# An attention block with a gated block behind it: background work that waits for a time of the plan

## The chip, the cores and the metric

The kernel runs on one core of a Trainium2 chip. The metric is the time of one execution on the device, in microseconds (us). A core has five engines that run side by side, each with its own queue of instructions that it takes in order: TensorE (PE in the profile; its weight loads are listed apart, as PEld), VectorE (DVE), ScalarE (ACT), GpSimd (POOL) and SyncE (SP), which here issues all transfers (DMA). They wait for each other through semaphores. An instruction that waits at the head of its engine's queue holds all that stand behind it.

## The reference

One sequence of 2048 rows of 640 numbers (bf16) goes through attention and then through a gated block:

```python
x = A_x
h = x + _A_ref(_layernorm(x, axis=-1), A_wqkv, A_wo)
h2 = h + _B_ref(_layernorm(h, axis=-1), B_w_gate, B_w_up, B_w_down)
```

`_A_ref` makes queries, keys and values for 32 heads of 20 numbers, the softmax of `q k^T / sqrt(20)`, its product with the values, and the product of all heads with `wo` (640 x 640). `_B_ref` is `((x w_gate) * (x w_up)) w_down`, with 1728 columns between. `_layernorm` takes off the mean and divides by the root of the variance.

## The kernel before

Heads are taken in 8 groups of 4; a head has a slot of 32 partitions. Queries are taken in 4 blocks of 512, in passes "0", "1", "2", "3" (block 3 is partly split into two halves "A" and "B"). Keys and values come in 16 tiles of 128 rows, four tiles to a chunk, so 4 chunks.

**The main loop** goes over 683 score tiles of 1536 columns (three units of 512, each one head by one key tile). `emit_S` has TensorE multiply keys with queries into one of two score tiles `sc` (L456). ScalarE takes the exponential of the tile into one of six buffers `E` (L469). Where the plan finds VectorE free (`x_takes`), the exponential covers 1024 columns only and VectorE works out the last 512 in five instructions (`emit_x`, L494 to L505). `emit_AV` multiplies the finished exponentials with the values into the one accumulator `acc` (L631); at the end of a group VectorE copies it out (L642, L647).

**Other work of TensorE** is a list of jobs that share one work bank `mi`: a job's matmuls, then VectorE's copy out of the bank, then the next job. Jobs are projections of queries and keys (`job_proj`, copied by L286), values (`job_V`, copied by L248), transposes of normalized input (`T_of`, `job_lnT`, copied by L248), and, when a block of queries is done, its output product (`out_mm`), the second layer norm and the gated block. Where the plan finds TensorE idle, two filler matmuls are issued (`keep_warm`, L432).

**Who sets the order.** The program is written out by a planner that runs while the kernel is built. It keeps its own clocks: `at["pe"]` and `at["dve"]` are the times in ns at which it believes TensorE and VectorE to be, advanced by fixed costs for each job. Nothing of these clocks is left on the chip: what they set is the order of instructions in each engine's queue. `run_job` and `spare` decide after each tile which jobs and which background work go next.

**VectorE's background work** is the list `aux` of generators. `step_aux` runs the first of them to its next `yield` and adds the yielded cost to `at["dve"]`; only when it is finished does the next get a turn. `ensure_aux` drives the list until a named thing is done. In the list are:

- `gen_ln(ch)` for chunks 1 to 3: four statistics (L183, L184) of the chunk's input `xs`, the inverse root of the variance in small steps on POOL (`rstd_steps`, L189 to L214), a reciprocal on VectorE (L219), then four times subtract and multiply (L238, L239). Between POOL's steps and the reciprocal the generator yields 24 times a cost of 50 ns. A chunk's input must have been asked for (`while ch not in xs`); `xs` has two buffers, so chunk 3's load (L142) waits until chunk 1's transposes have read theirs.
- `load_wo`: for each of 8 groups, clear `wo[g]` (L789) and issue four transfers of 20 rows each (L793).
- later, `ln2_pieces` of the second layer norm.

**Sums.** After L642 copies a group's accumulator to `asb`, `norm` stores its row of sums to DRAM and reads it back in another shape (L537, L538); five tiles later `back` puts the reciprocal into VectorE's queue (L543), and stores and spreads the result (L545, L548); eight tiles on, POOL multiplies (L554). `later(n, fn)` is "n tiles from now".

**The order of jobs in a chunk** (the loop over `ch`): for chunks 1 to 3 four values, then the keys of head groups 1, 2, 3, with the next chunk's transposes between; the key of group 0 was made at the end of the chunk before. A chunk's group takes 5.33 tiles, so the key of group 1 is wanted about five tiles after the chunk begins.

Of the kernel before, what the change touches and what calls it, by code (L numbers as in the profile page):

```python
# [33 lines left out]
TPB = QB // P  # L34
# [20 lines left out]
EXP_NS, EXP_END, EXP_COL = 50, 166, 5 / 6  # L55
S_NS, S_EXP, SWITCH, LAT = 323, 500, 110, 150
TOL, LEAST, MARGIN = 200, 430, 100
X_LEAST, X_OUT = 3, 6
E_BUFS = 6
SHIFT = 1184.0  # L60
# [12 lines left out]
def kernel(  # L73
# [112 lines left out]
    def rstd_steps(mv, n, made, ve_=None):  # L186
        ve_ = ve_ or nc.vector
        mb = small.tile([P, n], BF16, name="mb")
        ve_.tensor_copy(mb[:], mv[:, :, 0])  # L189
        m32 = small.tile([P, n], F32, name="m32")  # L190
        ve_.tensor_copy(m32[:], mb[:])
        vb = small.tile([P, n], BF16, name="vb")
        ve_.tensor_copy(vb[:], mv[:, :, 1])
        ve = small.tile([P, n], BF16, name="ve")
        ve_.tensor_scalar_add(ve[:], vb[:], EPS_B)
        v = small.tile([P, n], F32, name="v")
        ve_.tensor_copy(v[:], ve[:])
        yield 1000 if ve_ is nc.vector else 50
        y = small.tile([P, n], F32, name="y")
        ve_.tensor_scalar(y[:].bitcast(I32), v[:].bitcast(I32), -0.5, float(0x5F3759DF), ALU.mult, ALU.add)  # L200
        t = small.tile([P, n], F32, name="nt")
        for k in range(3):
            ve_.tensor_tensor(t[:], y[:], y[:], ALU.mult)
            if ve_ is nc.gpsimd:
                ve_.tensor_tensor(t[:], t[:], v[:], ALU.mult)
                ve_.tensor_scalar(t[:], t[:], -0.5, 1.5, ALU.mult, ALU.add)
                ve_.tensor_tensor(y[:], t[:], y[:], ALU.mult)
            else:
                ve_.scalar_tensor_tensor(t[:], t[:], -0.5, v[:], ALU.mult, ALU.mult)
                ve_.scalar_tensor_tensor(y[:], t[:], 1.5, y[:], ALU.add, ALU.mult)  # L210
            if k != 2:
                yield (800, 600)[k] if ve_ is nc.vector else 50
        den = small.tile([P, n], BF16, name="den")
        ve_.tensor_tensor(den[:], v[:], y[:], ALU.mult)  # L214
        if ve_ is nc.gpsimd:
            for _ in range(24):
                yield 50
        r = small.tile([P, n], F32, name="rstd")
        nc.vector.reciprocal(r[:], den[:])  # L219
        made.append((m32, r))  # L220
        yield 1000 if ve_ is nc.vector else 200
# [2 lines left out]
        nc.vector.tensor_scalar(dst, src, m32[:, k:k + 1], r[:, k:k + 1], ALU.subtract, ALU.mult)  # L224

    lns = {}
    now = {"i": 0}
    at = {"pe": 0, "dve": 0, "mi": 0, "acc": 0, "slot": [0, 0], "exp": 0, "av": {}}

    def dve(ns):  # L230
# [128 lines left out]
    def later(n, fn):  # L359
        events.append((now["i"] + n, fn))  # L360
# [45 lines left out]
                raise RuntimeError(f"no job for {key}")  # L406

    def step_aux():
        while aux:
            try:  # L410
                at["dve"] += next(aux[0]) or 200
                return True
            except StopIteration:
                aux.popleft()
        return False

    def spare(until):
# [2 lines left out]
                break  # L420

    def ensure_aux(key):
        while key not in done:
            if not step_aux():
                raise RuntimeError(f"nothing makes {key}")

    COST = {"T": 300, "v": 680, "nf": 780}

# [101 lines left out]
    def norm(s, asb):  # L530
# [6 lines left out]
        nc.sync.dma_start(sums[:], asb[DH:P:SLOT, 0:w])  # L537
        nc.sync.dma_start(r16, sums[:].rearrange("j (c f) -> (j c) f", f=n))  # L538

        def back():  # L540
            ri = nrm.tile([P, n], F32, name="ri", tag=f"ri{n}")
            dve(240)
            nc.vector.reciprocal(ri[:], r16)  # L543
            scr = dram.tile([HPG, w], F32, name="scr", tag=f"scr{w}")
            nc.sync.dma_start(scr[:].rearrange("j (c f) -> (j c) f", f=n), ri[:])  # L545
            bc = nrm.tile([P, QB], F32, name="bc")
            for j in range(HPG):
                nc.sync.dma_start(bc[SLOT * j:SLOT * (j + 1), 0:w], scr[j:j + 1, :].to_broadcast([SLOT, w]))  # L548

            def mult():  # L550
                if b and ("om", b - 1) not in done:
                    later(1, mult)
                    return
                nc.gpsimd.tensor_tensor(On[g][:, c0:c0 + w], asb[:, 0:w], bc[:, 0:w], ALU.mult)  # L554
                done.add(("n", p, g))
            later(8, mult)
        later(5, back)

    def sums_on_pe(asb, w):
        ps = bank()  # L560
# [192 lines left out]
    for ch in range(NB):  # L753
        nxt = deque(range((ch + 1) * TPB, (ch + 2) * TPB) if ch + 1 < NB else [])

        def one_T():
            if nxt:
                t = nxt.popleft()
                add(("T", t), T_of(t))
        def values():  # L760
            for t in range(ch * TPB, (ch + 1) * TPB):
                add(("v", t, 0), job_V(t, 0))
        if ch:
            values()
        for g in range(1, G1):
            if ch == 0:
                add(("q", 0, g), job_proj(0, g, 0))
            add(("k", g, ch), job_proj(1, g, ch))
            if ch == 0 and g == 1:
                values()  # L770
            if g > 1:
                one_T()
        one_T()
# [13 lines left out]
    def load_wo():  # L787
        for g in range(NG):
            nc.vector.memset(wo[g][:], 0.0)  # L789
            yield 230  # L790
            for j in range(HPG):
                h = HPG * g + j
                nc.sync.dma_start(wo[g][SLOT * j:SLOT * j + DH, :], A_wo[DH * h:DH * h + DH, :])  # L793

    def make_identf():
        nc.vector.tensor_copy(identf[:], ident[:])
# [477 lines left out]
```

## Time and profile before

| | |
|---|---|
| median of 3 runs | 968.78 us (967.51 to 969.49) |
| the profiled execution | 966.26 us |
| its span, first to last instruction | 964.4 us |
| ScalarE busy | 899.1 us (93%) |
| TensorE busy | 845.2 us (88%) |
| VectorE busy | 604.3 us (63%) |
| POOL busy | 59.8 us (6%) |
| granted TensorE clock, mean | 0.980 |

In the profile's rows, `L469 ACT ACTIVATE E<-sc` is line 469, ScalarE, the operation, and the tile written and read. In groups there follow the count, the busy time, the mean of one in ns, and the idle time of the engine just before them with what ended it. In a timeline the row begins with start and length in us, and idle time stands in brackets. In a table of stretches the busy times of the engines are followed by the granted clock of TensorE (1.00 is full speed), the DMA engines' share and the bytes moved per second.

### The profile page before, as it was taken

The numbers are of one execution on the slowest core, as the hardware profiler recorded it, in microseconds if no ns is written. First come the engines' busy times: TensorE is split into PE (matmuls) and PEld (weight loads), VectorE is DVE, ScalarE is ACT, GpSimd is POOL, SyncE is SP. The second block draws the span as 40 slices with busy tenths as digits, with TensorE's granted clock in tenths as the row PEclk, the third lists the DMA queues.
The fourth block names the chain that finished last, engine by engine and source line by source line (L and its number), as shares of the span: only waits on it lengthen the run. The fifth ranks groups of instructions, "written<-read, shape, count | busy, mean of one in ns | idle before, by whom it ended". The sixth has DMA issues, their size and how long they took to land.

```text
span 964.4 us, 18116 instructions
## 1 busy us (share of the span) xinstructions
PE 845.2 (88%) x7237; PEld 328.4 (34%) x7237; DVE 604.3 (63%) x1219; ACT 899.1 (93%) x719; POOL 59.8 (6%) x155
## 2 busy tenths in 40 slices
PE   7778999878988899998898999998898899888897
PEld 5233332222223222331233222332332334435465
DVE  7664448867778787888877887878644322133242
ACT  6889999979999899999999999999999999999941
POOL 3220011000000000000000000000000000000000
PEclk9999999989999999997999999999899999999899
DMA  6000010010060122004021221000502000202310
GB/s 185 28 1 1 1 29 22 15 44 12 3 186 13 40 77 51 20 27 182 13 68 39 68 68 33 27 27 15 155 2 67 14 13 20 62 23 59 76 41 17
DMA packets 67818, 44.44 MB, mean 46 GB/s; under 512 B 18504, under 2 KB 63404, under 8 KB 67728
## 3 DMA queue, kind: packets, MB, share of 16 engines
q1 hardware_dynamic: 67728, 43.23, 16.2%
q8 instruction: 58, 0.95, 0.4%
q14 instruction: 32, 0.26, 0.1%
HBM read 35.91 MB, written 7.30 MB: 45 GB/s over the span
## 4 chain that ended last, share of the span: by engine, by line
ACT 48%; PE 25%; issue 17%; DVE 8%; POOL 1%; DMA 1%; SPq 0%; ACTq 0%; DVEq 0%; POOLq 0%
ACT E L469 48%; PE sc L456 6%; PE acc L631 4%; PE mi L968 3%; PE mi L279 3%; PE mi L432 2%; PE f L913 2%; PE f L968 1%; PE mi L913 1%; PE mi L293 1%; DVE kT L286 1%; DVE st L183 1%; PE mi L847 1%; DVE xt L504 1%; DVE qa L286 1%
## 5 line engine op out<-in xcount | busy, mean ns | idle before, releaser
L469 ACT ACTIVATE E<-sc 128x1536 bf16<-128x1536 f32 (+1 forms) x683 | 881.7, 1466 | 24.6 <-PE sc L456 18.5
L456 PE MATMUL sc<-qa,kT 32*128 32x512 bf16 x1536 | 204.5, 389 | 49.8 <-ACT E L469 42.3
L456 PEld LDWEIGHTS <-kT 32*128 32x128 bf16 x2432 | 85.5, 91 | 297.1 <-issue 258.1
L631 PE MATMUL acc<-E,vx 128*32 128x512 bf16 (+1 forms) x2331 | 171.9, 355 | 1.4 <-DVE asb L642 0.9
L279 PE MATMUL mi<-lnT,wp 128*128 128x512 bf16 x310 | 85.3, 386 | 16.6 <-DVE qa L286 10.7
L494 DVE TENSOR_SCALAR xv<-sc 128x512 f32<-128x512 f32 x101 | 69.6, 689 | 41.0 <-PE sc L456 40.2
L456 PE MATMUL sc<-qb,kT 32*128 32x256 bf16 (+1 forms) x896 | 69.8, 293 | 16.2 <-ACT E L469 15.0
L554 POOL TENSOR_TENSOR on<-asb,bc 128x512 bf16<-128x512 f32 (+1 forms) x30 | 34.6, 1153 | 716.5 <-DMA bc<-scr 430.9
L504 DVE SCALAR_TENSOR_TENSOR xt<-xm 128x512 f32<-128x512 int32 x101 | 76.7, 759 | 2.1
L499 DVE SCALAR_TENSOR_TENSOR xe<-xt,xv 128x512 int16<-128x512 f32 x101 | 70.8, 701 | 1.7
L505 DVE SCALAR_TENSOR_TENSOR xt<-xt,xm 128x512 f32<-128x512 f32 x101 | 69.9, 692 | 2.1
L631 PEld LDWEIGHTS <-vx 128*32 128x32 bf16 x2432 | 45.0, 96 | 67.2 <-issue 66.4
L968 PE MATMUL mi<-wd,hh 128*128 128x320 bf16 x364 | 63.7, 303 | 1.5 <-DVE xr L972 1.5
L432 PE MATMUL mi<-kT,ident 128*128 128x512 bf16 x196 | 61.6, 397 | 2.1 <-DVE ln2T L248 1.0
L968 PEld LDWEIGHTS <-hh 128*128 128x128 bf16 x448 | 38.8, 98 | 37.4 <-issue 25.2
L913 PE MATMUL mi<-ln2T,wg 128*128 128x512 bf16 (+1 forms) x170 | 47.6, 387 | 3.7 <-DVE u L248 3.5
L921 DVE TENSOR_TENSOR hh<-mi,u 128x512 bf16<-128x512 f32 (+1 forms) x42 | 28.8, 687 | 34.9 <-PE mi L913 34.7
L913 PE MATMUL mi<-ln2T,wu 128*128 128x512 bf16 (+1 forms) x170 | 46.3, 382 | 3.9 <-DVE hh L921 3.9
L248 DVE CAST u<-mi 128x512 bf16<-128x512 f32 (+1 forms) x42 | 28.9, 688 | 32.7 <-PE mi L913 32.6
L279 PEld LDWEIGHTS <-wp 128*128 128x128 bf16 x310 | 26.2, 97 | 62.0 <-issue 46.8
L503 DVE TENSOR_SCALAR xm<-xv 128x512 int32<-128x512 int32 x101 | 44.1, 436 | 0.6
L847 PE MATMUL mi<-wo,on 128*128 128x320 bf16 x224 | 38.8, 301 | 2.3 <-DVE xr L851 2.2
(150 smaller groups left out, 610.3 us busy)
## 6 DMA issues: line engine op xcount, KB each, us to landing
bc<-scr SPq DMA_DIRECT2D x100, 64.0 KB
wu<-in_B_w_up_dram SPq DMA_DIRECT2D x20, 320.0 KB
wg<-in_B_w_gate_dram SPq DMA_DIRECT2D x20, 320.0 KB
qsp<-qa SPq DMA_DIRECT2D x8, 384.0 KB
xr<-in_A_x_dram SPq DMA_DIRECT2D x16, 160.0 KB
out_dram<-xr SPq DMA_DIRECT2D x14, 160.0 KB
wd<-in_B_w_down_dram SPq DMA_DIRECT2D x13, 160.0 KB
xs<-in_A_x_dram SPq DMA_DIRECT2D x3, 640.0 KB
```

The source lines that it names most:

```text
L279: nc.tensor.matmul(ps[:], lhsT=wslice(m, g, c), rhs=lnT[:, c, ch * QB:(ch + 1) * QB], start=(c == 0), stop=(c == KT - 1))
L432: nc.tensor.matmul(ps[:], lhsT=ident[:], rhs=kT[0][:, 0:BANK], start=True, stop=True)
L456: nc.tensor.matmul(sc[:, o:o + w], lhsT=kT[g][SLOT * j:SLOT * (j + 1), kt * P:(kt + 1) * P], rhs=q_of(g, b, c0, w)[SLOT * j:SLOT * (j + 1) ...
L469: exps = nc.scalar.activation(e[:, 0:n_act], sc[:, 0:n_act], ACT.Exp, bias=EXP_BIAS, scale=SM_SCALE)
L494: took = nc.vector.tensor_scalar(v[:], ps, X_SCALE, X_BASE, ALU.mult, ALU.max)
L499: nc.vector.scalar_tensor_tensor(e[:], t[:], X_C, v[:], ALU.add, ALU.add)
L504: (700, lambda: nc.vector.scalar_tensor_tensor(t[:], m[:], X_A, m[:], ALU.mult, ALU.mult)),
L505: (700, lambda: nc.vector.scalar_tensor_tensor(t[:], t[:], X_B, m[:], ALU.add, ALU.mult)),
L631: nc.tensor.matmul(acc["t"][SLOT * j:SLOT * (j + 1), 0:w], lhsT=vx[kt][:, VS * h:VS * h + SLOT], rhs=e, start=(acc["n"][j] == 0), stop=(ac ...
L847: nc.tensor.matmul(ps[:, 0:HALF], lhsT=on[g][:, t * P:(t + 1) * P], rhs=wo[g][:, cs], start=(g == 0), stop=(g == NG - 1))
L913: nc.tensor.matmul(ps[0:M, 0:n], lhsT=st["w", fp][k][:, c, f2 * P:f2 * P + M], rhs=st["ln2T"][:, c, c0:c0 + n], start=(c == 0), stop=(c == ...
L968: nc.tensor.matmul(ps[:, 0:HALF], lhsT=st["hh"][f][0:K, t * P:(t + 1) * P], rhs=late["Wd"][f][0:K, cs], start=(f == 0), stop=(f == 2 * FP ...
```

## The change

Four edits, all in the planner:

1. A generator of background work may yield `WAIT`, "not yet". `step_aux` then gives the next generator in the list a turn instead of stopping at the first. `ensure_aux` sets `now["forced"]`, under which no generator waits. The 24 yields before the reciprocal of the first layer norm become a wait until `at["pe"]` has passed the time of POOL's last step by `ROOT_NS` = 5000.
2. `load_wo` waits `WO_NS` = 1500 of the plan's time after each group of four transfers.
3. `back` is called four tiles after the sums are stored, and puts itself off by a tile at a time until `at["pe"]` has passed the store by `SUMS_NS` = 6000.
4. In chunks 1 to 3 two values stand ahead of the key of group 1, and two behind it.

```diff
+WO_NS, SUMS_NS, ROOT_NS = 1500, 6000, 5000
...
         if ve_ is nc.gpsimd:
-            for _ in range(24):
-                yield 50
+            due = max(at["dve"], at["pe"]) + ROOT_NS
+            while at["pe"] < due and not now["forced"]:
+                yield WAIT
...
     def step_aux():
-        while aux:
+        for gen in list(aux):
             try:
-                at["dve"] += next(aux[0]) or 200
+                c = next(gen)
+                if c == WAIT:
+                    continue
+                at["dve"] += c or 200
                 return True
             except StopIteration:
-                aux.popleft()
+                aux.remove(gen)
         return False
...
     def ensure_aux(key):
+        now["forced"] = True
         while key not in done:
             if not step_aux():
                 raise RuntimeError(f"nothing makes {key}")
+        now["forced"] = False
...
+        due = at["dve"] + SUMS_NS
+
         def back():
+            if at["pe"] < due and now["i"] < n_tiles:
+                later(1, back)
+                return
...
-        later(5, back)
+        later(4, back)
...
-        def values():
-            for t in range(ch * TPB, (ch + 1) * TPB):
+        def values(k=0, n=TPB):
+            for t in range(ch * TPB + k, ch * TPB + n):
                 add(("v", t, 0), job_V(t, 0))
         if ch:
-            values()
+            values(0, 2)
         for g in range(1, G1):
...
-            if ch == 0 and g == 1:
-                values()
+            if g == 1:
+                values(2 if ch else 0)
...
                 nc.sync.dma_start(wo[g][SLOT * j:SLOT * j + DH, :], A_wo[DH * h:DH * h + DH, :])
+            due = at["pe"] + WO_NS
+            while at["pe"] < due and not now["forced"]:
+                yield WAIT
```

2 lines of the change are left out of this document (1 added, 1 removed).

## The prediction

> **What bounds the kernel now.** I read the page first (busy shares and the chain of waits), then ScalarE's instructions by shape, the timeline of ScalarE for its gaps, and SyncE, VectorE and TensorE where the gaps lie.
>
> ```profile
> PE 845.2 (88%) x7237; PEld 328.4 (34%) x7237; DVE 604.3 (63%) x1219; ACT 899.1 (93%) x719; POOL 59.8 (6%) x155
> ...
> ACT 48%; PE 25%; issue 17%; DVE 8%; POOL 1%; DMA 1%; SPq 0%; ACTq 0%; DVEq 0%; POOLq 0%
> ```
>
> ```profile
> L469 ACT ACTIVATE E<-sc 128x1536 bf16<-128x1536 f32 x581 | 804.9, 1529 | 17.6 <-PE sc L456 14.3 <-PE acc L631 1.7
> L469 ACT ACTIVATE E<-sc 128x1024 bf16<-128x1024 f32 x102 | 113.2, 1110 | 7.0 <-PE sc L456 4.1 <-PE acc L631 2.6
> ```
>
> ScalarE is busy 93% of the span. Its 683 exponentials (581 whole, 102 with a third taken over by VectorE) run back to back almost everywhere; before them it was idle 24.6 us in all. I number them from 0. So a change can win only what closes a gap of ScalarE, or takes columns off it. Its timeline shows where the large gaps are (start, length, engine, instruction; in brackets the idle time before it):
>
> ```profile
> 28.66 2.79 ACT L469 ACTIVATE E<-sc 128x1536 bf16<-128x1536 f32 x2 [1.73 <-PE acc L631]
> 32.96 14.88 ACT L469 ACTIVATE E<-sc 128x1536 bf16<-128x1536 f32 x11 [1.50 <-PE sc L456]
> 48.67 6.82 ACT L469 ACTIVATE E<-sc 128x1536 bf16<-128x1536 f32 x5 [0.83 <-PE sc L456]
> 59.73 21.60 ACT L469 ACTIVATE E<-sc 128x1536 bf16<-128x1536 f32 x16 [4.24 <-PE sc L456]
> ```
>
> ```profile
> 209.47 3.88 ACT L469 ACTIVATE E<-sc 128x1024 bf16<-128x1024 f32 x3 [3.96 <-PE sc L456]
> 214.60 2.36 ACT L469 ACTIVATE E<-sc 128x1536 bf16<-128x1536 f32 x2 [1.25 <-PE sc L456]
> 217.32 18.44 ACT L469 ACTIVATE E<-sc 128x1536 bf16<-128x1536 f32 x14 [0.36 <-PE sc L456]
> ```
>
> ```profile
> 319.69 3.71 ACT L469 ACTIVATE E<-sc 128x1024 bf16<-128x1024 f32 x3 [2.11 <-PE acc L631]
> ```
>
> Two groups can be touched by the edits: 8.30 us before exponentials 8, 10, 21 and 26 (start), and 5.57 us between 205.5 and 217.3 us (the output weight).
>
> **Part 1, the output weight's transfers and the read-back.** SyncE's queue, then VectorE and TensorE at the second group:
>
> ```profile
> 191.21 11.93 SPq L793 DMA_DIRECT2D wo<-in_A_wo_dram  x32
> 203.24 0.51 SPq L537 DMA_DIRECT2D sums<-asb  x1
> ```
>
> ```profile
> 206.68 0.25 DVE L543 RECIPROCAL ri<-sums_all 128x16 f32<-128x16 f32 x1 [4.45 <-DMA sums_all<-sums]
> 206.85 0.69 DVE L286 TENSOR_SCALAR qa<-mi,shift_row 128x512 bf16<-128x512 f32 x1
> ```
>
> ```profile
> 207.59 1.23 PE L279 MATMUL mi<-lnT,wp 128*128 128x512 bf16 x4 [3.78 <-DVE qa L286]
> ```
>
> The reader is to see a line of four. The 32 transfers hold SyncE for 11.93 us; the sums that L537 stores are issued only after them, at 203.24; the reciprocal that reads them back stands in VectorE's queue and waits 4.45 us; behind it stands the copy that frees TensorE's one work bank, so TensorE waits 3.78 us and ScalarE 3.96 us. In the order of the changed kernel's built instructions the sums stand behind 4 of the 32 transfers instead of all, and the reciprocal follows five exponentials behind the store (in the order before the two stand within one). Store to landing took 3.44 us (203.24 to 206.68), five exponentials take over 6 us (14 in 18.44 us above), so the wait should be gone: **-3.96 us**. The two gaps of 1.25 and 0.36 us behind it lie in and after a stretch in which TensorE had half its clock, quoted under the rivals, that began when it had stood still; without the stop I take them as gone too: **-1.61 us**. Bounds for this part: -5.57, and 0 if another wait takes the place.
>
> The transfers stay 32 and the clearing of wo 8 memsets; only their spread changes (the last group is issued about exponential 145 instead of 135). Their first reader stands near exponential 194 in the changed order, so that costs nothing; without that cover one late group would be a wait of four issues, 11.93 / 8 = 1.49 us. On SyncE, 28 of the 32 come behind the stored sums, and the read-back results (L545, L548, five issues) stand between groups; one group ahead is 1.49 us, below the slack of the multiply on POOL eight exponentials later. Of the other 33 read-backs no reciprocal waits for its DMA in the trace of before; they move by at most four exponentials. I take 0 for them, between 0 and one more wait like the 4.45.
>
> **Part 2, roots and second keys at the start.** VectorE before exponentials 8 to 10 with the first half of a normalizing pair, the copies of chunk 1's first and second keys with a statistic between, and one value's matmuls on TensorE:
>
> ```profile
> 26.14 0.49 DVE L248 CAST vx<-mi 128x320 bf16<-128x320 f32 x1 [0.93 <-PE mi L293]
> 29.52 0.18 DVE L219 RECIPROCAL rstd<-den 128x4 f32<-128x4 bf16 x1 [2.89 <-POOL den L214]
> 29.62 0.72 DVE L286 TENSOR_SCALAR qa<-mi,shift_row 128x512 bf16<-128x512 f32 x1
> ```
>
> ```profile
> 32.34 0.38 DVE L238 TENSOR_SCALAR xs<-xs,m 128x640 bf16<-128x640 bf16 x1
> ```
>
> ```profile
> 47.37 0.75 DVE L286 TENSOR_SCALAR kT<-mi,one_row 128x512 bf16<-128x512 f32 x1 [0.80 <-PE mi L279]
> ```
>
> ```profile
> 57.45 0.88 DVE L183 BATCH_NORM_STATS2 st<-xs 128x6 f32<-128x320 bf16 x2
> 58.36 0.21 DVE L184 BATCH_NORM_AGGREGATE mv<-st 128x2 f32<-128x12 f32 x1
> 58.49 0.70 DVE L286 TENSOR_SCALAR kT<-mi,one_row 128x512 bf16<-128x512 f32 x1
> ```
>
> ```profile
> 48.71 0.85 PE L293 MATMUL mi<-wv,lnT 128*128 128x320 bf16 x5
> ```
>
> First root (times of the changed kernel, here and below, are estimates from these rows). Now the reciprocal stands ahead of the query's copy and holds it to 29.62. In the new order it stands behind that copy and the accumulator's; in its place are two statistics of the next chunk (0.88 + 0.21 each), already loaded. They delay the value copy by 0.26 us, the projection behind it ends near 28.2, the copy near 28.95, the key's projection near 30.3; the key's copy waits on VectorE to 30.7 for the reciprocal and one normalizing pair (twice 0.38), and ends at 31.4. Exponential 10 starts near 31.9 instead of 32.96: -1.0.
>
> Chunk 1's first key. The list of background work now steps past a generator that waits, so the statistics of chunk 3 come early: in the new order two of them stand right behind the issue of that chunk's load and ahead of the copy of kT[0] (47.37 above). They must wait for the load:
>
> ```profile
> 44.05 0.37 SPq L142 DMA_DIRECT2D xs<-in_A_x_dram  x1
> ```
>
> ```profile
> 47.00:48.00 1.00, 0.65 (x3) 0.09 (x1) 0.63 (x1) 0.84 (x1) 0.76 (x5) 1.00 0.68 248
> 48.00:49.00 1.00, 0.82 (x8) 0.33 (x9) 0.12 (x1) 0.33 (x1) 0.67 (x5) 1.00 0.00 0
> ```
>
> The load is issued at 44.05, as soon as the last transposes of the tile before it have left its buffer, and its bytes flow until 48.0 (248 GB/s in the microsecond before, 0 after): 3.95 us. The new order puts one more score group ahead of those transposes, so the issue stays near 43.9 despite the 1.0 us won, and the load lands at 47.85. Two statistics pairs (2.2) and the key's copy (0.75) end at 50.8; exponential 21 starts at 51.3 instead of 48.67: +2.6.
>
> Second key, exponential 26. From 51.5: value 0.85, its copy 0.49, root and two normalizing pairs 1.7, the accumulator's copy 0.7 (as long as the key's), second value's copy 0.49 (55.9); the key's five matmuls with a score and a value group between them 2.5 (58.4); VectorE meanwhile two pairs and one statistic to 58.6; copy 0.70, scores 0.4: 59.9 instead of 59.73. Two values and their 1.4 us each are no longer ahead of the key, but the late chunk start eats what that wins. Sum at exponential 26: **+0.2 us**. Bounds: -2.3 if chunk 3's statistics don't hold the key (the same steps from 47.7 give 57.4), +3 if, with two values now behind the key, exponentials 28 to 32 wait again.
>
> **Part 3, the shape of the plan.** Counted in the built order: 103 tiles instead of 101 give a third to VectorE, each taking 1529 - 1110 = 0.42 us off ScalarE: **-0.84 us**, paid by VectorE, busy 63%. Filler matmuls of L432 fall from 196 to 160. Everything from exponential 676 on stands in the same order, so the tail of some 41 us costs what it did. In between the order is dealt anew; the gap of 2.11 us at 319.69 may go or come back elsewhere: 0, between -2 and +2.
>
> **Sum.** -5.57 - 0.84 + 0.2 = -6.2 us. The profiled execution took 966.26 us (span 964.4 and 1.9 around it), so its like would take 960.1. The median of the three runs, 968.78, lies 2.5 above it; against the median the forecast is 962.6 us.
>
> **Rivals.** The half-clock stretches bear on one of them (stretch, its length, busy times of PE, PEld, DVE, ACT, POOL, granted clock, DMA share, GB/s; then the stretches ahead of the first and of the fifth):
>
> ```profile
> 208.28:215.10 6.82, 6.73 (x31) 1.40 (x29) 3.60 (x7) 4.32 (x4) 1.65 (x1) 0.50 0.16 41
> 276.54:279.96 3.42, 3.42 (x18) 0.48 (x16) 2.98 (x5) 2.98 (x3) 0.00 (x0) 0.50 0.87 278
> 320.92:324.33 3.41, 3.41 (x18) 0.65 (x16) 0.00 (x0) 2.52 (x3) 0.00 (x0) 0.50 0.03 5
> 436.97:447.21 10.24, 9.21 (x51) 1.52 (x50) 7.19 (x12) 9.78 (x8) 0.00 (x0) 0.50 0.84 316
> 692.97:699.80 6.83, 6.59 (x42) 2.59 (x38) 2.90 (x6) 6.14 (x5) 0.00 (x0) 0.50 0.01 2
> 908.01:914.84 6.83, 6.83 (x54) 3.50 (x49) 0.99 (x4) 5.98 (x5) 0.00 (x0) 0.50 0.69 183
> ```
>
> ```profile
> 204.87:208.28 3.41, 0.69 (x4) 0.29 (x3) 1.56 (x4) 0.64 (x1) 0.00 (x0) 1.00 0.05 5
> ...
> 689.56:692.97 3.41, 2.39 (x25) 1.41 (x24) 3.08 (x7) 3.41 (x4) 0.00 (x0) 1.00 0.89 262
> ```
>
> (a) Slower: the clock. 36 fewer fillers leave TensorE quieter, and it falls to half clock more often. In the last five stretches ScalarE's idle time was 0.44, 0.89, 0.46, 0.69 and 0.85, 0.67 us each. To end 0.2% above before, 6.2 + 1.9 = 8.1 us must be lost: 13 new stretches, of at most 18 places where a pair of fillers is gone; all 18 give 962.6 + 12.0 = 974.6. For it: the stretch at 208 follows one with TensorE 20% busy. Against it: the fillers go where the plan puts other matmuls instead. 6%.
> [...]
>
> (b) The stall comes back: VectorE, with copies and its thirds of the scores, can't keep pace once the pause at 205 is gone, and ScalarE waits there as long in small gaps. 5.57 lost again: 968.2, no change. For it: VectorE's busiest stretches before.
>
> ```profile
> 175.00:200.00 25.00, 20.64 (x155) 6.22 (x154) 21.71 (x40) 24.12 (x20) 1.40 (x1) 1.00 0.16 34
> ```
>
> Against it: with VectorE busy 21.71 of 25 us ScalarE still had 24.12. 8%.
>
> (c) The start wins after all: chunk 3's load or its statistics don't hold the key. -2.3 instead of +0.2: 960.1. 15%.
>
> (d) The start loses the 3 us of its upper bound: 965.4. 13%.
>
> **How the numbers follow.** Forecast 58%, (c) 15%, (d) 13%, (b) 8%, (a) 6%. A measurement of this kernel can tell about 0.2%, 1.9 us. Faster holds the forecast, (c) and (d): 0.86; same (b): 0.08; slower (a): 0.06. The range leaves (a) and (b) out and reaches past (c) and (d) by the spread of the runs and half of part 3's: 958.5 to 967.0.
>
> **What would show it.** Right: no wait of a reciprocal on sums_all above 1 us, no ScalarE gap over 1 us near exponential 136, a new gap of about 4 us before exponential 21 with VectorE waiting for xs ahead of the copy of kT[0], and a gap near 1 us instead of 4.24 before 26. Wrong: the 21 gap missing (then c), gaps at 28 to 32 (d), more half-clock stretches between 150 and 700 us (a), or many small gaps behind the scores' third on VectorE (b).

## The result, and the profile after

The changed kernel took 957.73 us (median of 4 runs, 957.24 to 958.26) and the kernel before, run beside it, 969.13 (4 runs, 967.51 to 972.19): a ratio of 0.9887, 95% interval 0.986 to 0.9913. Run again later it took 958.71 us (6 runs, 957.2 to 959.5) against 968.70, a ratio of 0.991 (0.9888 to 0.9932). The direction was forecast with 0.86. The first median lies 0.8 us below the range of 958.5 to 967.0 and 4.9 below the forecast of 962.6; the later one lies just inside the range. The profiled execution took 958.26 us, its span 956.4, its mean granted clock 0.979.

The page of the changed kernel, then ScalarE's exponentials by shape (count, busy time, mean of one in ns, idle time ahead of them):

```profile
PE 837.3 (88%) x7201; PEld 327.1 (34%) x7201; DVE 610.7 (64%) x1229; ACT 897.8 (94%) x719; POOL 59.8 (6%) x155
```

```profile
L476 ACT ACTIVATE E<-sc 128x1536 bf16<-128x1536 f32 x579 | 801.0, 1522 | 15.9 <-PE sc L463 12.8 <-PE acc L643 1.7 <-ACT E L476 0.2
L476 ACT ACTIVATE E<-sc 128x1024 bf16<-128x1024 f32 x104 | 114.6, 1102 | 2.1 <-PE sc L463 1.0 <-PE acc L643 0.9
```

ScalarE is as busy as before (897.8 against 899.1 us). What went is its idle time: ahead of the exponentials 18.0 us instead of 24.6. (The profile names 104 short exponentials where 103 tiles were counted, as it named 102 for 101 before.)

**The output weight.** SyncE's queue, the reciprocal on VectorE and ScalarE's timeline at the place where the stop was:

```profile
196.11 1.41 SPq L805 DMA_DIRECT2D wo<-in_A_wo_dram  x4
197.71 0.52 SPq L544 DMA_DIRECT2D sums<-asb  x1
199.43 0.35 SPq L545 DMA_DIRECT2D sums_all<-sums  x1
199.88 2.92 SPq L805 DMA_DIRECT2D wo<-in_A_wo_dram  x8
...
207.59 8.45 SPq L805 DMA_DIRECT2D wo<-in_A_wo_dram  x20
```

```profile
204.03 0.24 DVE L555 RECIPROCAL ri<-sums_all 128x16 f32<-128x16 f32 x1
```

```profile
189.05 27.97 ACT L476 ACTIVATE E<-sc 128x1536 bf16<-128x1536 f32 x22
217.18 5.05 ACT L476 ACTIVATE E<-sc 128x1536 bf16<-128x1536 f32 x4 [0.15 <-PE sc L463]
```

Four transfers stand ahead of the stored sums instead of 32, the reciprocal waits for nothing (no bracket in its row), and ScalarE works 27.97 us without a gap where it had stood 3.96, 1.25 and 0.36 us.

**The start.** ScalarE's timeline, VectorE ahead of the copy of kT[0], SyncE's issue of chunk 3's load, and the microseconds around its landing (busy times of PE, PEld, DVE, ACT, POOL, granted clock, DMA share, GB/s):

```profile
28.34 17.82 ACT L476 ACTIVATE E<-sc 128x1536 bf16<-128x1536 f32 x13 [1.73 <-PE acc L643]
50.65 4.13 ACT L476 ACTIVATE E<-sc 128x1536 bf16<-128x1536 f32 x3 [4.50 <-PE sc L463]
55.85 2.79 ACT L476 ACTIVATE E<-sc 128x1536 bf16<-128x1536 f32 x2 [1.06 <-PE sc L463]
59.54 4.13 ACT L476 ACTIVATE E<-sc 128x1536 bf16<-128x1536 f32 x3 [0.91 <-PE sc L463]
```

```profile
47.15 0.89 DVE L184 BATCH_NORM_STATS2 st<-xs 128x6 f32<-128x320 bf16 x2 [3.67 <-DMA xs<-in_A_x_dram]
...
49.19 0.70 DVE L288 TENSOR_SCALAR kT<-mi,one_row 128x512 bf16<-128x512 f32 x1
```

```profile
42.98 0.37 SPq L143 DMA_DIRECT2D xs<-in_A_x_dram  x1
```

```profile
46.00:47.00 1.00, 0.00 (x0) 0.00 (x0) 0.00 (x0) 0.15 (x1) 0.00 (x0) 1.00 0.53 195
47.00:48.00 1.00, 0.00 (x0) 0.00 (x0) 0.85 (x2) 0.00 (x0) 0.00 (x0) 1.00 0.00 0
```

The 13 exponentials from 28.34 us on are one stretch: the gap of 1.50 us before exponential 10 is gone. Before exponential 21 stands a new gap of 4.50 us. VectorE waits 3.67 us for `xs`, and two statistics stand ahead of the key's copy. Between 46 and 47 us TensorE, VectorE and GpSimd do nothing, and ScalarE only the end of one exponential, while the load's bytes flow (195 GB/s). The second key's gap (exponential 26) fell from 4.24 to 0.91 us; a new one of 1.06 us stands before exponential 24, in a half-clock stretch (48.61 to 55.44 us).

**The middle.** One place is different that no edit names. Before, ScalarE stood 2.11 us at 319.69 and 0.89 us at 324.29. In the first of these gaps it waited for products of TensorE, which waited for VectorE's copy of the accumulator (VectorE, then TensorE, before):

```profile
318.45 0.69 DVE L642 COPY asb<-acc 128x512 f32<-128x512 f32 x1
319.20 0.62 PE L631 MATMUL acc<-E,vx 128*32 128x512 bf16 x8 [0.85 <-DVE asb L642]
```

TensorE still had its full clock there; the half-clock stretch at 320.92 came behind. In the changed kernel ScalarE works through:

```profile
299.25 24.49 ACT L476 ACTIVATE E<-sc 128x1536 bf16<-128x1536 f32 x19
323.97 11.36 ACT L476 ACTIVATE E<-sc 128x1024 bf16<-128x1024 f32 x9 [0.23 <-PE sc L463]
```

The idle time of ScalarE ahead of its exponentials, added over ranges of them (gaps of 0.05 us and more, in us):

| exponentials | before | after | difference |
|---|---|---|---|
| 1 to 30 (start) | 8.30 | 8.69 | +0.39 |
| 31 to 130 | 1.26 | 1.30 | +0.04 |
| 131 to 145 (output weight) | 5.75 | 0.15 | -5.60 |
| 146 to 560 (middle) | 6.03 | 3.27 | -2.76 |
| 561 to 675 | 0.22 | 2.70 | +2.48 |
| 676 to 682 (end) | 1.84 | 0.93 | -0.91 |
| all, and the first with 0.66 | 24.07 | 17.71 | -6.36 |

With 1.3 us less of ScalarE's busy time this gives -7.7 of the 8.0 us between the two spans (964.4 and 956.4). The other 0.3 us stand ahead of the first exponential, which began at 16.04 us before and at 15.71 after.

### The profile page after: what moved, and what is told of

It reads as the page before. It is cut to its first block, busy times and chain, and to the rows that moved or that the text cites. A ratio compares the mean times of both kernels' runs of the same rounds, so it can differ in the third digit from the quotient of the medians.

```text
span 956.4 us, 18055 instructions
## 1 busy us (share of the span) xinstructions
PE 837.3 (88%) x7201; PEld 327.1 (34%) x7201; DVE 610.7 (64%) x1229; ACT 897.8 (94%) x719; POOL 59.8 (6%) x155
## 4 chain that ended last, share of the span: by engine, by line
ACT 47%; PE 26%; issue 17%; DVE 9%; DMA 0%; ACTq 0%; DVEq 0%
ACT E L476 47%; PE sc L463 6%; PE acc L643 4%; PE mi L281 3%; PE mi L983 3%; PE mi L928 2%; PE mi L295 2%; PE f L928 2%; PE mi L439 1%; PE f L983 1%; PE mi L946 1%; DVE kT L288 1%; DVE vx L250 1%; DVE qa L288 1%; DVE st L184 1%
## 5 line engine op out<-in xcount | busy, mean ns | idle before, releaser
L506 DVE SCALAR_TENSOR_TENSOR xe<-xt,xv 128x512 int16<-128x512 f32 x103 | 77.2, 749 | 1.3
L439 PE MATMUL mi<-kT,ident 128*128 128x512 bf16 x160 | 50.0, 395 | 0.9 <-DVE vx L250 0.3
L862 PE MATMUL mi<-wo,on 128*128 128x320 bf16 x224 | 40.8, 308 | 3.4 <-DVE xr L866 3.2
```

The costliest lines, as they stand in the source:

```text
L439: nc.tensor.matmul(ps[:], lhsT=ident[:], rhs=kT[0][:, 0:BANK], start=True, stop=True)
L506: nc.vector.scalar_tensor_tensor(e[:], t[:], X_C, v[:], ALU.add, ALU.add)
```

## The experiments

Theory: the stop at the output weight is made by SyncE's line of 32 transfers ahead of the stored sums; edit 2 or edit 3 takes it away; edits 1 and 4 win at the start what chunk 3's statistics then lose; and the rest of the gain lies in the middle. Against it stand the prediction's rivals. The shares of ScalarE's idle time below are formed as in the table above. In the diffs, "edit 1" to "edit 4" are those of the change.

### The kernel before and the changed kernel, run again

No edit.

> The kernel before once more, unchanged, for a second trace of it. The profiled executions differ by 8.0 us in span (964.4 and 956.4), the medians by 11.4 us (969.13 and 957.73). Theory A (the gaps of the two traces are typical, the rest is where these runs of before happened to fall): the ScalarE gap before exponential 136 is again 3.96 us within 0.3, and its time lies within 965 to 970. Theory B (the stop at the output weight varies and is longer in the slower runs): in a run near 969 the gap before exponential 136 is 5 to 8 us. Theory C (half-clock stretches vary): the gap is 3.96, and the sum of gaps between exponentials 141 and 560 is over 7 us instead of 5.65.

967.78 us (12 runs, 965.14 to 972.51), ratio to the other runs of before 0.9987 (0.9967 to 1.0008). The span of this profile is 969.6 us, 5.2 longer than that of the first, with the same program: ScalarE's idle time is 28.42 us instead of 24.07, of which 1.84 more at the start and 1.37 more in the middle (7.40), while the gap before exponential 136 is 4.28 instead of 3.96; and TensorE had half its clock for 51.2 us of the time up to 920 us instead of 37.5. Over 19 runs beside it before took from 964.13 (mean clock 0.980) to 974.13 us (0.964). So one execution of this kernel can lie 4 us below the median of these runs (968.23) or 6 us above it.

> The changed kernel once more, for a second trace and more times. Two traces of before, spans 964.4 and 969.6, differ in the half-clock stretches of TensorE and the gaps of ScalarE beside them, while the gap at the output weight is 3.96 and 4.28. Theory (half-clock stretches make the spread, in both kernels): the times of the changed kernel spread over several us too, the gaps before exponentials 21 and 26 are again 4.5 and about 1, and the ratio to before moves up from 0.9887, to 0.989 to 0.992. Rival (the changed kernel has lost what made before spread): its times stay within 957 to 959.

958.71 us (6 runs, 957.2 to 959.5), span 956.3. The gap before exponential 21 is 4.69 us, the stop at the output weight 0.07, the middle 4.62 and the range behind it 2.42 us (together 7.04, against 6.90 in the first profile of it). The changed kernel is the steadier of the two: its ten runs spread over 2.3 us. Why is open; it has 37.5 and 41.0 us at half clock up to 920 us in its two profiles.

### Output weight: the transfers on another queue

```diff
-                nc.sync.dma_start(wo[g][SLOT * j:SLOT * j + DH, :], A_wo[DH * h:DH * h + DH, :])
+                nc.gpsimd.dma_start(wo[g][SLOT * j:SLOT * j + DH, :], A_wo[DH * h:DH * h + DH, :])
```

On the kernel before; GpSimd issues the 32 transfers, nothing else is touched.

> The kernel before with one word changed: the 32 transfers of the output weight are issued by POOL instead of SyncE; the order on VectorE, ScalarE and TensorE stays. Theory queue (the sums stand behind the 32 issues): sums are stored at about 197 us, the reciprocal does not wait, the gaps 3.96, 1.25 and 0.36 go, 5.6 us faster than before (ratio 0.994). Rival transfers (the DMA engines are full with the weight): the reciprocal still waits 3 us or more, within 0.2% of before.

963.25 us (7 runs), ratio 0.9938 (0.9913 to 0.9962). The 32 transfers now take 16.30 us of GpSimd's queue, the reciprocal waits for nothing, and ScalarE has no gap at their place:

```profile
190.91 16.30 POOL L793 DMA_DIRECT2D wo<-in_A_wo_dram  x32 [6.76 <-DVE wo L789]
```

```profile
197.20 39.20 ACT L469 ACTIVATE E<-sc 128x1536 bf16<-128x1536 f32 x31 [0.55 <-PE sc L456]
```

With no change in the plan this shows the cause of the stop: SyncE's line, as the prediction read it. The ratio means 6.0 us of 968.2. The trace itself is only 2.7 us shorter than the first of before: its middle has 10.78 us of idle time instead of 6.03: the gap at exponential 219 is 3.94 us instead of 2.11, in a half-clock stretch of 13.65 us (309.6 to 323.3).

### Edit 2 alone

```diff
+            due = at["pe"] + WO_NS
+            while at["pe"] < due and not now["forced"]:
+                yield WAIT
```

On the kernel before, with the new `step_aux` and `ensure_aux`.

> The kernel before with the spacing of the output weight's transfers alone (and the list of background work that steps past a waiting generator, which it needs). Start and read-back as before. Theory of the prediction: the start's gaps stay at 8.3 us, the gap before exponential 136 goes, 5.6 us faster (ratio 0.994), plus or minus 2 for the newly dealt order. Rival: the whole 11.4 us come from this one stop, ratio 0.988.

963.06 us (7 runs), ratio 0.9934 (0.991 to 0.9958). The stop is gone (131 to 145: 0.29 us); the start is that of before (8.31). The middle has 8.61 us, again with 3.94 at exponential 219 in a half-clock stretch of 13.65 us.

### Edit 3 alone

```diff
+        due = at["dve"] + SUMS_NS
+
         def back():
+            if at["pe"] < due and now["i"] < n_tiles:
+                later(1, back)
+                return
...
-        later(5, back)
+        later(4, back)
```

> The kernel before with the read-back of sums by time alone. The 32 transfers still hold SyncE, but the reciprocal stands two exponentials later, so its wait should fall from 4.45 to about 1.8 us and the ScalarE gap from 3.96 to about 1.5. The second layer norm and the gated block of the first query block begin at exponential 193 and 223 instead of 191 and 217. Theory re-dealt middle (that shift is what takes away the 2 to 4 us before exponential 219): the gap there is below 0.5, 5 to 6 us faster than before (ratio 0.994). Rival: a gap of over 1.5 us stays between exponentials 210 and 230, 2.5 us faster.

961.91 us (6 runs), ratio 0.994 (0.9917 to 0.9964). Here all 32 transfers still stand ahead of the sums:

```profile
194.29 11.92 SPq L799 DMA_DIRECT2D wo<-in_A_wo_dram  x32
206.31 0.51 SPq L538 DMA_DIRECT2D sums<-asb  x1
208.01 0.35 SPq L539 DMA_DIRECT2D sums_all<-sums  x1
```

```profile
209.77 0.25 DVE L549 RECIPROCAL ri<-sums_all 128x16 f32<-128x16 f32 x1 [0.56 <-DMA sums_all<-sums]
```

The reciprocal waits 0.56 us instead of 4.45, because it is put into VectorE's queue later. The sums are just as late as before; nothing stands behind them that matters. ScalarE's idle time in 131 to 145 is 0.38 us. (1.08 us came at exponential 129, in a half-clock stretch; the 0.55 us at exponential 130 are there before too.) The gap at exponential 219 is gone, and the middle has 2.79 us.

### The changed kernel without edit 2

```diff
-            due = at["pe"] + WO_NS
-            while at["pe"] < due and not now["forced"]:
-                yield WAIT
```

> The changed kernel without the spacing of the output weight's transfers. In the run of the read-back alone the stop at the output weight was gone too, though all 32 transfers stood ahead of the sums (gaps 1.08 and 0.55 stayed at 129 and 130). Theory both (either edit is enough): the gaps between exponentials 126 and 145 add up to under 2.5 us, 958 to 960, as the changed kernel. Rival (here the order is dealt so that the reciprocal comes early, at 134): a gap of 4 us or more there, 963.

964.22 us (12 runs), ratio 0.9968 (0.9954 to 0.9983). Twelve transfers stand ahead of the sums, the reciprocal waits 0.23 us, and ScalarE runs through:

```profile
189.03 40.84 ACT L476 ACTIVATE E<-sc 128x1536 bf16<-128x1536 f32 x32
```

So for the stop at the output weight edit 2 and edit 3 are two remedies for one ailment: each alone takes it away, and both together take it away once. Yet this kernel is some 6 us slower than the changed one. 0.84 us of it are two thirds fewer on VectorE (101). The rest lies elsewhere: its middle has 6.95 us of idle time, where the changed kernel has 3.27 and 4.62, and ScalarE is busy 900.0 us instead of 897.8. Its gated block begins behind exponential 220, that of the changed kernel behind 223.

### The start: edit 4 alone, edit 1 alone

Edit 4 as in the change, on the kernel before:

```diff
         if ch:
-            values()
+            values(0, 2)
...
-            if ch == 0 and g == 1:
-                values()
+            if g == 1:
+                values(2 if ch else 0)
```

> The kernel before with two values behind the second key instead of ahead of it, alone. Chunk 3's statistics stay late here. Theory of the prediction: gaps before 8, 10 and 21 stay at 1.73, 1.50 and 0.83, the one before 26 falls from 4.24 to about 1.8 us; the stop at the output weight stays at 3.96. The middle is dealt as in the changed kernel (193 and 223): no gap over 0.5 before exponential 219. Sum: 2.4 + 2 to 3, 4.4 to 5.5 us faster (ratio 0.995). Rival (values behind the key hold the exponentials 28 to 32): the gaps of the start add up to 8.3 again.

Median 963.05 us of 12 runs that spread from 960.85 to 970.37; the ratio, 0.9971 (0.9949 to 0.9992), is worth 2.8 us. The second key's gap fell from 4.24 to 0.53 us; exponential 21 lost 2.29, in a half-clock stretch that began at 44.7:

```profile
49.81 6.82 ACT L469 ACTIVATE E<-sc 128x1536 bf16<-128x1536 f32 x5 [2.29 <-PE sc L456]
57.16 4.13 ACT L469 ACTIVATE E<-sc 128x1536 bf16<-128x1536 f32 x3 [0.53 <-PE sc L456]
```

The stop at the output weight stands (6.94 us in 131 to 145, 5.75 before). The gated block begins behind exponential 223 here too; the gap at 219 is gone, and the middle has 3.33 us.

Edit 1 alone, on the kernel before, with the new `step_aux` and `ensure_aux`:

```diff
-            for _ in range(24):
-                yield 50
+            due = max(at["dve"], at["pe"]) + ROOT_NS
+            while at["pe"] < due and not now["forced"]:
+                yield WAIT
```

> The kernel before with the wait for the first layer norm's root alone (and the list that steps past it). Theory of the prediction, its steps without the moved values: the gap before exponential 10 falls from 1.50 to about 0.2, the one before 21 rises from 0.83 to about 4.5 (chunk 3's statistics stop VectorE on their load), and the second key stands behind four values of 1.4 us each, so the gap before 26 is about 4; the start's gaps add up to 10.5 to 11.5 instead of 8.3, 2 to 3 us slower than before. Rival (the time won at 10 is kept): 8.3 or less, no slower.

970.86 us (12 runs), ratio 1.003 (1.0011 to 1.0049): slower. The wait for chunk 3's load is there (3.68 us on VectorE, 4.63 before exponential 21), and with four values still ahead of the second key its gap is 3.90:

```profile
52.34 4.13 ACT L476 ACTIVATE E<-sc 128x1536 bf16<-128x1536 f32 x3 [4.63 <-PE sc L463]
...
64.17 12.20 ACT L476 ACTIVATE E<-sc 128x1536 bf16<-128x1536 f32 x9 [3.90 <-PE sc L463]
```

Its start has 12.66 us of idle time against 8.30 before. So in these traces edit 1 alone costs 4.4 us at the start, of which 1.24 stand before exponential 13 in a half-clock stretch and 1.00 before exponential 24 behind another; its times say 2.9 us. Edit 4 wins 3.7 at the second key.

### Chunk 3's statistics held until its load is there

```diff
-        while ch not in xs:
-            yield 1330
+        if ch not in xs:
+            while ch not in xs:
+                yield WAIT
+            due = at["pe"] + LOAD_NS          # 7000
+            while at["pe"] < due and not now["forced"]:
+                yield WAIT
```

On the changed kernel. The generator that had to wait for its load gives way to the next for 7 us of the plan.

> The changed kernel, in which chunk 3's statistics wait 7000 ns of the plan after the issue of that chunk's load. Theory: in the changed kernel VectorE stops on that load ahead of the copy of kT[0]; here the gap before exponential 21 falls from 4.50 to about 0.8 us, the one before exponential 26 stays below 1.5, 2.5 us faster than the changed kernel, about 955.2. Rival (the second key is late whatever the statistics do, so what is won at 21 is lost at 26): the gaps up to exponential 30 add up to the same 8.6 us, 957.7.

954.51 us (6 runs, 952.50 to 956.98), ratio to before 0.9846 (0.9821 to 0.987): 3 to 4 us below the changed kernel, and faster than both. The copy of kT[0] now stands ahead of the statistics and waits for TensorE alone; the gap of 4.50 is 0.82:

```profile
45.53 0.75 DVE L288 TENSOR_SCALAR kT<-mi,one_row 128x512 bf16<-128x512 f32 x1 [3.09 <-PE mi L281]
```

```profile
46.83 4.13 ACT L476 ACTIVATE E<-sc 128x1536 bf16<-128x1536 f32 x3 [0.82 <-PE sc L463]
51.69 2.90 ACT L476 ACTIVATE E<-sc 128x1536 bf16<-128x1536 f32 x2 [0.73 <-PE sc L463]
55.45 4.14 ACT L476 ACTIVATE E<-sc 128x1536 bf16<-128x1536 f32 x3 [0.86 <-PE sc L463]
```

The start has 4.64 us of idle time instead of 8.69: the 4 us that the load's wait cost.

### Fillers: none, and more

The changed kernel without its 160 filler matmuls (the clock, rival a):

```diff
     def keep_warm():
-        ps = bank()
-        for _ in range(2):
-            nc.tensor.matmul(ps[:], lhsT=ident[:], rhs=kT[0][:, 0:BANK], start=True, stop=True)
+        pass
```

> The changed kernel without its 160 filler matmuls; the plan and the order of all else stay. Rival (a) of the prediction, the clock: without them TensorE falls to half clock in more stretches (over 12 instead of 9), ScalarE waits 0.67 us more for each, 2 to 6 us slower than the changed kernel. Against it: the stretches follow windows that the fillers do not reach; the same number of stretches, within 1 us of the changed kernel.

969.45 us (12 runs), ratio 1.0016 (0.9997 to 1.0036): 10.7 us above the changed kernel run beside it, all that the change had won. The mean granted clock is 0.907. Two half-clock stretches, each behind the 3.41 us ahead of it:

```profile
435.29:438.70 3.41, 2.06 (x22) 0.62 (x20) 3.34 (x7) 3.41 (x4) 0.00 (x0) 1.00 0.63 235
438.70:489.90 51.20, 41.32 (x247) 7.66 (x247) 38.19 (x65) 49.65 (x41) 3.04 (x2) 0.50 0.32 107
...
646.92:650.33 3.41, 1.74 (x20) 0.46 (x16) 3.34 (x7) 3.41 (x4) 0.66 (x1) 1.00 0.38 127
650.33:677.64 27.31, 21.90 (x131) 3.81 (x129) 23.25 (x37) 26.71 (x22) 2.38 (x2) 0.50 0.18 48
```

In the first of them, 51.20 us long, ScalarE was still busy 49.65 us: half clock costs it little where TensorE has room (busy 41.32 us of the 51.20). Up to 920 us the half clock came to 177.5 us instead of 37.5. The spans differ by 11.1 us; if all of it is put down to the half clock, 3.41 us of it cost 11.1 / 140.0 * 3.41 = 0.27 us here. The rival's mechanism is real, but its condition did not come: the changed kernel has 37.5 us at half clock, as many as before.

More fillers, on the kernel with held statistics: a pair is issued where the plan has 400 or 600 ns less room than it asked for before.

```diff
-            if i > WARM and not ran and cur["fresh"] and idle < at["slot"][-2] + TOL:
+            if i > WARM and not ran and cur["fresh"] and idle < at["slot"][-2] + FILL_TOL:
```

> The changed kernel with chunk 3's statistics held, and fillers already where the plan leaves 400 ns less room: 202 fillers instead of 160. Without its 160 fillers the changed kernel took 10.7 us more, in half-clock stretches. Theory clock: more fillers take away more of these stretches, 1 to 3 us faster than with the statistics held alone (954.5). Rival (the stretches left follow bursts of loads and not idle time): 954 to 956.

> The same with 600 ns, 224 fillers. Theory clock: as fast as with 202 or faster, fewer half-clock stretches. Rival: fillers begin to stand ahead of score matmuls, many gaps of 0.1 to 0.3 us, 1 us or more slower than with 202.

With 202 fillers 958.37 us (6 runs), with 224 963.23 (10 runs), against 954.51 with 160. The half clock up to 920 us fell from 47.8 to 34.1 us in both, but ScalarE's idle time in the middle rose from 5.25 to 8.50 and 8.62 us. What of it lies away from the half-clock stretches (over 2 us behind one) rose from 1.79 to 3.63 and 4.28. That fits fillers that stand as late work in front of the scores, but it isn't shown: the order of other jobs also changed with them, so the 8.7 us of the last are not all a price of fillers.

### The middle: where the gated block begins

One number of the kernel before, the pause ahead of the first block's output product, so that its gated block begins behind exponential 223 as in the changed kernel (before: 217):

```diff
-            add(("pause",), slots(3))
+            add(("pause",), slots(7))
```

> The kernel before with one number changed: the pause ahead of the first query block's output product is 7 places of the plan instead of 3. In the built order the output product then begins behind exponential 194 instead of 191 and the gated block behind 223 instead of 217, as in the changed kernel; start, transfers and read-back are those of before. Theory (the middle's gain is only where the gated block's first matmuls lie against the accumulator's copy at the end of a group, which stands near exponential 216): the gap of 2 to 4 us before exponential 219 is gone, ScalarE's idle time over exponentials 146 to 560 is 2.8 to 5.3 us instead of 5.8 to 7.4, the stall near 136 stays at 4 to 6 us, and the time is about 3 us below before (ratio near 0.997). Rival (the middle's idle time is dealt anew by chance with any change of order): no gap at 219, but the sum over 146 to 560 stays at 6 or more, and the time is that of before within 0.2%.

966.39 us (12 runs), ratio 0.9987 (0.9969 to 1.0004): 1.3 us less, and an interval that also holds no change. The gap at exponential 219 is gone:

```profile
298.59 32.53 ACT L469 ACTIVATE E<-sc 128x1536 bf16<-128x1536 f32 x25
```

The middle's idle time is 5.67 us, above the 2.8 to 5.3 expected. Parted by the clock: away from half-clock stretches it is 1.48 us, where the two profiles of before had 3.26 and 3.39; in them and within 2 us behind, it is 4.19 against 2.78 and 4.01. So in the traces the later start of the gated block is worth about 1.8 us, near the gap of 2.11, and what the clock makes of the middle comes on top. The times don't show that gain: as the rival expected, they are within 0.2% of before.

The changed kernel with the same number moved the other way (gated block behind 220, 101 thirds, 194 fillers):

```diff
-            add(("pause",), slots(3))
+            add(("pause",), slots(2))
```

> The changed kernel with the same number at 2 instead of 3: the gated block begins behind exponential 220 instead of 223 (before: 217), with 101 thirds on VectorE instead of 103 and 194 fillers instead of 160. Theory: a gap of 1 to 4 us stands again between exponentials 215 and 230, the sum over 146 to 560 is 6 or more instead of 3.3 to 4.6, and with 0.84 us for the two thirds the time is 3 to 5 us above the changed kernel, about 962.5. Rival: the start tile of the gated block has no price; the sum stays at 3 to 5 and only the two thirds are lost, 959.6.

965.61 us (12 runs), ratio 0.9971 (0.9953 to 0.999): 7 to 8 us above the changed kernel, more than either side expected, and close to the 964.22 of the kernel without edit 2, whose gated block begins at 220 too. The profile is that of the slowest of the twelve (968.32 us). The gap is back, cut in four:

```profile
299.49 14.60 ACT L476 ACTIVATE E<-sc 128x1536 bf16<-128x1536 f32 x11
315.00 1.45 ACT L476 ACTIVATE E<-sc 128x1536 bf16<-128x1536 f32 x1 [0.91 <-PE acc L643]
316.90 1.02 ACT L476 ACTIVATE E<-sc 128x1024 bf16<-128x1024 f32 x1 [0.45 <-PE sc L463]
318.15 1.45 ACT L476 ACTIVATE E<-sc 128x1536 bf16<-128x1536 f32 x1 [0.23 <-PE sc L463]
320.42 10.00 ACT L476 ACTIVATE E<-sc 128x1536 bf16<-128x1536 f32 x8 [0.82 <-PE sc L463]
```

The next fence is this kernel's table of stretches, the one behind it the changed kernel's about one exponential further on:

```profile
309.32:312.73 3.41, 1.08 (x11) 0.49 (x10) 3.27 (x7) 3.41 (x4) 0.00 (x0) 1.00 0.00 0
312.73:319.55 6.82, 6.19 (x35) 1.82 (x36) 3.44 (x7) 5.23 (x5) 0.00 (x0) 0.50 0.02 4
```

```profile
308.01:311.42 3.41, 2.65 (x22) 0.81 (x21) 2.92 (x16) 3.41 (x4) 0.00 (x0) 1.00 0.03 5
```

TensorE was busy 1.08 of 3.41 us while ScalarE was still busy throughout; then TensorE had half its clock, and the gaps lie in and just behind that stretch. In the changed kernel TensorE has 2.65 us of work there, among it four fillers, and keeps its clock. Ahead of the first gap TensorE also waited for VectorE, busy 3.27 of the 3.41 us, first for a third of the scores (`xe`), then for the accumulator's copy:

```profile
312.83 0.61 PE L643 MATMUL acc<-xe,vx 128*32 128x512 bf16 x2 [0.99 <-DVE xe L506]
314.29 1.04 PE L643 MATMUL acc<-E,vx 128*32 128x512 bf16 x8 [0.31 <-DVE asb L654]
```

So VectorE's lateness and the half clock add up in this gap; no run parts them. The middle has 9.37 us, of which 6.89 lie in or behind half-clock stretches (58.0 us of them up to 920, against 37.5 and 41.0 in the two profiles of the changed kernel). That points at how empty the plan leaves TensorE in single stretches (busy 1.08 of 3.41 us here, 2.65 in the changed kernel). Why a move of three exponentials fills or empties so many of them, and costs 7 to 8 us, is open.

## Why the prediction was right, and where it failed

**Right: Part 1.** -5.57 was forecast and -5.60 measured, by the mechanism named (SyncE's line, shown by moving it to another queue). The 1.25 and 0.36 us behind the stop went with it, as taken. The prediction named both remedies as parts of one cure and did not see that either is enough: edit 3 alone does it with all 32 transfers in the way.

**Right: Part 2.** The steps came out nearly one by one: -1.0 at exponential 10 (the whole gap of 1.50 went), "a new gap of about 4 us before exponential 21 with VectorE waiting for xs" (4.50, with 3.67 on VectorE), "a gap near 1 us instead of 4.24 before 26" (0.91). The 1.06 us before exponential 24 were not forecast. The load was issued at 42.98 instead of the 43.9 taken, so exponential 21 started at 50.65 instead of 51.3. The sum of the start was put at +0.2 and is +0.39. Rivals (c) and (d) fell; what (c) would have won, 2.5 us against the forecast, the held statistics win, and more (4.05).

**Right against the rivals (a) and (b).** Neither the clock nor small gaps took the gain. The five stretches in (a) lost 3.33 us in 30.73 us at half clock, 0.37 us for each 3.41 us, against 0.27 without fillers; its upper bound for all 18 places, 12.0 us, is near the 10.7 us that leaving out all fillers cost. In the trace of the kernel without fillers the half clock at 438.70 began behind 3.41 us in which TensorE was busy 2.06 us, so here it came without TensorE standing still throughout.

**Wrong: two steps.** The first, and larger, is the last sentence of the sum: "The median of the three runs, 968.78, lies 2.5 above it; against the median the forecast is 962.6". It carried the place of one profiled execution among the runs of before over to the changed kernel. The changed kernel's profile, 958.26, lies 0.5 above its median; that is 3.0 us of the 4.9 us missed. The kernel before goes from 964.13 us at a mean granted clock of 0.980 to 974.13 at 0.964, and its first profile was one of its shorter executions. The runs of the changed kernel keep within 2.3 us. An error bound of some 4 us for the reference belonged into the range.

The other 1.8 us lie between the two profiles, 8.0 us where 6.2 were forecast. The largest part is a term that Part 3 put at nothing: "Everything from exponential 676 on stands in the same order, so the tail of some 41 us costs what it did". The order is the same, but from the start of exponential 676 to the end it took 53.39 us instead of 54.13 (53.40 instead of 54.17 in the second profiles), and ScalarE's idle time there fell from 1.84 to 0.93 us. The half-clock stretch near the start of this tail was 3.41 us long instead of 6.83, in both pairs of profiles. The same order was no reason for the same cost; what shortens that stretch is open. What remains are ScalarE's busy time (1.3 us less instead of 0.84), 0.3 us ahead of the first exponential and 0.3 in between, less the 0.2 us by which the start cost more than forecast.

**Right by luck.** "In between the order is dealt anew; the gap of 2.11 us at 319.69 may go or come back elsewhere: 0, between -2 and +2". From exponential 146 to 675 the idle time changed by -0.28 us, the sum of -2.76 and +2.48. In the second profiles it is -2.31 (8.46 and 6.15). The gap at 219 went and did not come back in either. Away from the half clock the middle fell from 3.26 to 2.07 us (3.39 to 1.81 in the second profiles), in and behind half-clock stretches from 2.78 to 1.20 (4.01 to 2.81).

The +2.48 has a part that belongs to the kernel. TensorE, then ScalarE, ahead of exponential 629 of the changed kernel:

```profile
835.27 1.78 PE L862 MATMUL mi<-wo,on 128*128 128x320 bf16 x6
836.99 0.41 PE L463 MATMUL sc<-qb,kT 32*128 32x256 bf16 x6
```

```profile
837.53 5.51 ACT L476 ACTIVATE E<-sc 128x1536 bf16<-128x1536 f32 x4 [1.14 <-PE sc L463]
```

Six matmuls of an output product stand ahead of the scores and take 1.78 us, most of it in a half-clock stretch (833.7 to 837.1). This gap, 1.02 to 1.34 us, stands in eight of the nine traces of kernels with edit 3, each time in or just behind a half-clock stretch, and in none of the seven without. So it goes with the order that edit 3 deals; by which of its moves is not shown. The prediction took 0 for "the other 33 read-backs" that edit 3 moves.

## What to carry to other kernels

When background work may step past a waiting item, look at what now runs early: here work whose input had only just been asked for took the place ahead of a copy on the critical path, and holding it for the load's time won another 3 to 4 us. An in-order queue's line (32 short transfers, 11.93 us) can be cured where it stands or where its result is awaited; check whether two edits cure the same stop before adding their gains. And set a forecast against the median only after several profiles of the same program: here two of them differ by 5.2 us.

## What the runs showed of the hardware

In the first two profiles the half-clock stretches, the last one of an execution aside, are 3.41, 6.83 or 10.24 us long; two of the kernel without fillers are 27.31 and 51.20 us long. How long TensorE was busy in the 3.41 us ahead of each one in the first two profiles, all at full clock:

| profile | half clock begins at, us | TensorE busy ahead of it, us of 3.41 |
|---|---|---|
| before | 208.28 | 0.69 |
| before | 276.54 | 1.53 |
| before | 320.92 | 1.49 |
| before | 436.97 | 1.51 |
| before | 692.97 | 2.39 |
| before | 908.01 | 2.07 |
| after | 48.59 | 0.78 |
| after | 277.29 | 1.94 |
| after | 441.13 | 1.84 |
| after | 509.39 | 2.23 |
| after | 683.47 | 2.26 |
| after | 833.66 | 1.87 |
| after | 857.55 | 2.07 |
| after | 901.93 | 1.68 |

So TensorE stood still throughout ahead of none of them. Nor does its busy time alone tell where the half clock comes: in the profile of before it was busy 1.81 us from 27.37 to 30.78, and the 3.41 us that follow are at full clock. What decides it is not shown.

In the two profiles of before the stretches begin at different places: after the first 50 us at 208.3 and 209.8, 276.5 and 278.1, 320.9 and 322.4 us, and the second has others at 32.3 and 46.0 that the first lacks. Half clock up to 920 us is 37.5 us in the first and 51.2 in the second, whose span is 5.2 us longer. Leaving out all 160 fillers brought the half clock from 37.5 to 177.5 us and cost 10.7 us. None of this tells why 64 more cost 8.7 us as well (with an order that also changed).
